# One core, attention and an expert layer: idle products moved to the head of TensorE's queue, one DMA for the last part of q, and new tables of order, engine and buffer

## The chip, the core and the metric

The kernel runs on one core of one Trainium2 chip. The metric is the time of one execution on the device in microseconds. Five engines work side by side, each through its own queue in order: PE (matrix products; its weight loads are listed as PEld), DVE, ACT, POOL (elementwise work), and SP, which here only issues DMAs. A queue whose next instruction waits holds back all that stands behind it.

## What is computed

```python
def _attn_ref(q, k, v):                      # q, k, v: (4, 8, 1152, 64)
    q_pool = q.reshape(B, H, S // 2, 2, D).mean(axis=3)
    scores = (1 / sqrt(D)) * np.matmul(q_pool, k.transpose(0, 1, 3, 2))
    scores = scores - np.max(scores, axis=-1, keepdims=True)
    attn = np.exp(scores)
    attn = attn / (np.sum(attn, axis=-1, keepdims=True) + 1e-09)
    return np.matmul(attn, v)
def _moe_ref(x, w_in, w_out):                # x: (2304, 512), 512 -> 2048 -> 512
    h = x @ w_in
    g = np.where(h > 0.0, h, np.exp(np.minimum(h, 0.0)) - 1.0)
    return g @ w_out
```

The weights come as float64 and are decoded on the chip.

## The kernel before, in words

There are four units, one for each batch, and each has four pairs of heads. A pair has nine score steps (two heads by four tiles of 128 pooled rows, and one of 64 rows from each head). A step is: `scores` on PE into the PSUM tile `s`, of which there is one; `biggest` on DVE, which reads `s`, finds the row maximum and writes `ep`; `expo` on ACT; `recip` (two operations on one column) on DVE or POOL. So the next `scores` waits until `biggest` has read the last one.

After that a step goes one of two ways. In a "split" pair (eleven of sixteen) the numbers are turned into two float16 parts, `phi` (hb, on ACT, POOL or DVE) and `plo` (DVE), DMAs transpose them, and `pv_split` multiplies them with v. In the others PE transposes `ep` (`turn`), ACT or DVE copies it out (`out_act`), and `pv` multiplies in float32. The first two pairs are "plain" as well: q and k stay float32, `q_twice` adds the two q rows of a pool, PE transposes them (`flip_turn`) and `flip_out` copies them out. For the other pairs `q_sum`, `hi` and `lo` make float16 halves.

The expert layer works on half a unit at a time (256 and 320 rows): `xlo` ends its input, 16 groups of products `m1_all` give h, six elementwise steps (`neg`, `ex`, `em`, `join`, `gh`, `gl`) give g, and `m2_all` makes the output, which `oe` copies out and `od` stores. Before that the weights are decoded on DVE (`dec`, three operations, 32 times) and split in two parts (`w_hi`, `w_lo`).

None of this runs in loops on the chip. The program makes 2691 tasks, and the table `ORDER` gives the order in which they are written out: `943v` is task 943 on DVE (p is PE, a ACT, g POOL, s a DMA on SP). What stands in front of a task on the same letter is what that engine does first. Many tasks can run on more than one engine, and the letter picks one. `SLOTS` says which buffer of its kind each value gets. The durations that `plan.add` is given are for the search that made the tables; with the tables written out they reach no instruction.

At the head of the kernel: `load_k` on SP, `load_qa` twice and `load_qb` (two DMAs, one for each head) on ACT's queue; `q_twice` three times on DVE, the third for `load_qb`'s part; `flip_turn` and `flip_out`; the first `scores`. Task 0 is `warm`, six products of the identity with itself, whose result nobody reads.

Of the kernel before, what the change touches and what calls it, by code (L numbers as in the profile page):

```python
# [37 lines left out]
411v 430g 41g 483p 484v 44a 359s 445p 446a 456p 468p 469a 304s 412p 473p 457a 295v 466p 474v 298s
498a 499g 467a 46p 447p 315v 47v 311v 413a 475a 519p 284s 448a 476v 297a 464p 454p 504p 48a 520v
449v 465a 49g 424p 485a 52a 300v 455a 505a 303s 509p 500p 510v 306v 481p 317a 487p 482a 502p 477p  # L40
555p 501a 50s 511a 488a 302a 503a 521a 470p 556v 478a 24s 55s 542p 479p 557a 480a 525p 471a 526a
308s 51s 318s 425a 506p 305v 286v 543v 515p 489p 507a 426v 508v 472v 486v 287a 490v 369s 532p 516a
307a 558g 559p 533v 522v 517p 523p 527p 491p 544a 524a 518a 565p 310v 56v 492a 493p 534a 53g 566v
371v 54s 59a 494a 567a 538p 578p 573p 560a 528a 513p 495v 569p 539a 574a 579v 57s 360s 550p 570a
320v 43s 375s 563p 561p 514a 562a 564a 551a 60a 601p 546p 571p 535g 568g 548p 536p 602v 61p 322a
361v 547a 364s 588p 512g 529p 572a 580a 62v 63a 67a 603a 589v 537a 530a 614p 64v 365s 377v 581v
615v 575p 531v 576v 312a 323v 577v 65s 70s 582p 605p 637p 590a 66s 545v 583a 604g 549a 606a 68g
638v 594p 607p 608a 609p 324p 584p 585a 610a 69s 616a 540p 647p 611p 366v 325v 541a 595a 648v 373a
596p 586p 618p 587a 326p 649a 367v 624p 552p 597a 327v 639a 625v 328g 683p 626a 612v 650v 591v 640v
613v 684v 362v 592p 651p 72s 619a 593a 652a 645p 653p 655p 354s 656a 685a 75a 646a 620p 660p 621a  # L50
553a 661v 654a 329v 598p 670p 687p 330v 599a 554v 600v 617g 71g 628p 632p 344s 662a 629a 633a 671v
74a 641p 643p 630p 644a 622p 631v 627v 623v 686g 73s 76a 350s 693p 58s 363a 379s 694v 634p 663v
355s 356v 331g 332g 333v 672a 635v 642a 368a 334g 335g 336g 688a 691p 729p 657p 730v 695a 658a 689p
706p 731a 636v 659v 697p 664p 77p 1831v 690a 692a 665a 666p 674p 707v 78v 668p 716p 669v 673v 676p
698a 675a 667a 717v 701p 696g 708a 677a 79a 337v 357v 349s 733p 699p 678p 679a 700a 83a 718a 702a
734a 739p 680p 732v 740v 681v 719v 80v 710p 714p 735p 712p 713a 741a 715a 736a 752p 682v 338a 753v
352v 703p 84g 765p 704a 711a 709g 705v 766v 722p 747p 754a 88s 723v 374s 345s 755v 742v 1832v 737p
743p 756p 775p 776v 81s 82s 748a 744a 745p 758p 358a 757a 738a 759a 339g 340g 351v 724p 746a 720p
721a 777a 767a 85s 760p 761a 1833p 1834v 798p 725a 799v 90s 749p 376v 1837a 380s 762p 750a 1838v
778g 788p 783p 800a 789v 751v 353a 771p 378a 726p 784a 727a 763v 764v 341v 811p 769p 728v 801g 779p  # L60
781p 790a 770a 89g 796p 772a 773p 812v 806p 780a 86g 87v 768g 92a 824p 782a 807a 792p 774a 91s 785p
825v 381v 342g 791g 797a 813a 826a 793a 832p 804p 802p 815p 93a 814v 827v 803a 805a 816a 828a 347v
833v 1839p 834a 382v 819p 817p 820a 842p 794p 786a 818a 821p 835v 843v 787v 1840a 94a 346v 850p
836g 95p 1853p 844a 830s 838s 96v 829v 1867p 795a 384v 348a 831s 822a 97g 845v 101a 1835v 1841a
1842a 98v 1907v 1843v 383a 851v 99s 1868a 1869a 1854a 1855a 837v 823v 106s 1856a 808p 809v 810v
1908v 385v 860p 846a 852a 343g 861v 839s 1846p 386p 848s 1844g 104a 102g 1857v 853v 1858a 108s
1909p 868p 1870v 862a 1910v 847v 1859g 1881p 869v 387v 105v 863v 1847a 1848a 849s 1849g 388g 1845g
1913a 1850v 1871v 854a 389v 107v 100s 1888p 1889a 1890a 870a 1860p 1861a 1862a 1874p 103s 855v
1914v 878p 1851a 1863a 1864v 864a 840p 856s 1852g 1929p 879v 390a 857s 109s 871g 1875a 391v 392g
872g 865v 1876a 867s 906p 1891a 841a 1877a 907v 866s 1878v 393v 110a 1865a 880a 881g 1901p 874s  # L70
1892v 1879a 886p 111a 112a 394a 873v 887v 882a 395v 1895p 858p 875s 896p 859a 888a 883v 113p 908a
1866g 1872a 1893a 114v 115g 897v 396g 1896p 884s 885s 116v 889v 1930a 124s 1911v 1894v 914p 876p
909g 890a 1902p 397v 891v 898a 1882a 1931a 877v 1883a 1932g 892s 915v 1933v 1884g 910a 893s 1880g
1943p 912s 1934a 932p 916a 1885v 1935g 894p 117s 1950p 911v 899v 933v 398a 399v 917g 913s 900a 902s
895a 119a 118s 901v 918a 934a 903s 1836v 1951a 1873v 400a 1952a 919v 1922p 1923a 1924a 942p 1903p
920s 1953a 1944a 120v 1945a 1946a 921s 401v 943v 1897p 924p 121s 935v 936g 1925a 1947v 904p 1954v
944a 1886g 922p 1887g 925v 950p 1948a 1926v 402a 905a 1957p 1936p 923a 926a 937v 938s 1949v 122a
951v 939s 968p 1964p 952a 1937a 1938a 126s 927v 928v 403v 929v 945v 946g 1927a 1939a 1940v 969v
1941a 930s 1942g 1928g 931s 123v 1904p 947v 948s 953g 125g 129a 1965a 1958a 1905a 1966a 970a 954a
# [258 lines left out]
def attention_moe_kernel(  # L338
# [9 lines left out]
    nc = tc.nc  # L348
# [59 lines left out]
    def dve(n):  # L408
        return Port(1.08 * n + 75.0)
# [974 lines left out]
```

## Time and profile before

| | us |
|---|---|
| median of 3 runs | 742.1 (742.02 to 743.98) |
| the profiled execution, its own time | 742.65 |
| its span, first to last instruction | 740.9 |
| PE busy | 717.3 (97%) |
| DVE busy | 625.0 (84%) |
| ACT busy | 560.6 (76%) |
| POOL busy | 338.0 (46%) |

The span is told from the first instruction of the program to its last; 1.75 us of the execution lie around it. A busy PE is not a PE at its peak: products overlap, and their ends are modelled. What shows whether PE has work is the idle time before its instructions, and what ended it.

### The profile page before, as it was taken

The page shows a single profiled execution, that of the slowest core. Times are in us where ns is not written, and L with a number is a line of the kernel's source. Part 1 is how long each engine was busy: PE and PEld are TensorE (multiplying, and loading weights), DVE is VectorE, ACT ScalarE, POOL GpSimd, SP SyncE. Part 2 cuts the span into 40 slices and gives each one's busy share as a digit, 9 for nine tenths or more (in the row PEclk, how much of TensorE's full clock was granted, in tenths as well). Part 3 has the DMA queues.
Part 4 walks back from the last instruction along what each step waited for, and adds up shares of the span by engine and source line. Part 5 has one row for each costly group of instructions (what it writes and reads, how often), then busy time and mean ns, then how long its engine had stood idle before and what let it go on. Part 6 is the DMA issues. An engine that isn't in the chain of part 4 may idle for free.

```text
span 740.9 us, 19632 instructions
## 1 busy us (share of the span) xinstructions
PE 717.3 (97%) x7905; PEld 478.8 (65%) x7905; DVE 625.0 (84%) x1098; ACT 560.6 (76%) x974; POOL 338.0 (46%) x385
## 2 busy tenths in 40 slices
PE   5899998999999999999999999999999999999997
PEld 4577776877565555775676566786665665865753
DVE  6999999999998998879898879899988989875330
ACT  3899997998998887777688766889788564752651
POOL 1322455466626633376465554354646452440430
PEclk9999999999999999999999999999999999999999
DMA  8787834577999998999999999899899998793001
GB/s 304 287 228 251 247 119 105 142 135 160 171 179 207 178 204 169 211 181 174 213 171 208 189 205 181 163 162 209 173 189 194 188 162 137 139 139 64 30 1 36
DMA packets 310971, 126.01 MB, mean 170 GB/s; under 512 B 286304, under 2 KB 288352, under 8 KB 310880
## 3 DMA queue, kind: packets, MB, share of 16 engines
q1 hardware_dynamic: 310432, 124.16, 82.4%
q8 instruction: 62, 1.02, 0.6%
q10 hardware_dynamic: 448, 0.59, 0.2%
q14 instruction: 29, 0.24, 0.1%
HBM read 45.09 MB, written 4.72 MB: 67 GB/s over the span
## 4 chain that ended last, share of the span: by engine, by line
PE 47%; DVE 3%; ACT 2%; issue 1%; DVEq 0%; ACTq 0%
PE r L1310 16%; PE r L1229 14%; PE r L1119 6%; PE s L956 4%; PE s L970 3%; PE r L1101 1%; DVE ep L985 1%; PE r L1067 1%; ACT ep L991 1%; PE s L961 0%; DVE ep L1045 0%; DVE tmp L1265 0%; DVE x L1207 0%; DVE g L1291 0%; ACT hb L1042 0%
## 5 line engine op out<-in xcount | busy, mean ns | idle before, releaser
L991 ACT ACTIVATE ep<-ep,wk 128x1152 f32<-128x1152 f32 x136 | 170.4, 1254 | 45.7 <-DVE ep L985 40.5
L1229 PE MATMUL r<-x,wi 128*128 128x256 f16 (+1 forms) x1536 | 196.6, 286 | 1.5 <-DVE tmp L1265 1.5
L985 DVE TENSOR_SCALAR_CACHE_REDUCE ep<-s,sm 128x1152 f32<-128x1152 f32 x122 | 172.3, 1412 | 13.0 <-PE s L970 9.2
L1229 PEld LDWEIGHTS <-wi 128*128 128x128 f16 x1536 | 147.6, 98 | 43.6 <-issue 6.1
L1310 PE MATMUL r<-wo,g 128*128 128x512 f16 (+1 forms) x864 | 174.9, 380 | 0.1
L1045 DVE SCALAR_TENSOR_TENSOR ep<-ep,wk,hb 128x1152 f16<-128x1152 f32 x99 | 146.0, 1478 | 6.7 <-ACT hb L1042 4.7
L1310 PEld LDWEIGHTS <-g 128*128 128x128 f16 (+1 forms) x864 | 73.3, 100 | 83.8 <-issue 4.7
L956 PE MATMUL s<-kT,qT 128*128 128x512 f16 (+3 forms) x420 | 82.9, 328 | 4.3 <-DVE ep L985 3.3
L1119 PEld LDWEIGHTS <-v 128*64 128x64 f16 x2970 | 77.8, 110 | 11.4 <-issue 10.5
L1119 PE MATMUL r<-pT,v 128*64 128x128 f16 (+1 forms) x2970 | 84.4, 215 | 0.3 <-DVE tmp L1265 0.3
L1283 POOL TENSOR_TENSOR g<-tmp,g 128x320 f16<-128x320 f32 (+1 forms) x61 | 68.1, 1118 | 36.0 <-ACT g L1279 34.4
L499 POOL TENSOR_SCALAR wk<-wk 128x1 f32<-128x1 f32 x68 | 31.2, 459 | 114.3 <-ACT ep L991 93.9
L1042 ACT ACTIVATE hb<-ep,wk 128x1152 f16<-128x1152 f32 x50 | 62.3, 1249 | 17.3 <-POOL wk L1010 8.2
L1036 POOL TENSOR_SCALAR hb<-ep,wk 128x1152 f16<-128x1152 f32 x34 | 44.3, 1303 | 56.6 <-DVE wk L1001 29.6
L1265 DVE SCALAR_TENSOR_TENSOR tmp<-r,tmp 128x320 f32<-128x320 f32 (+1 forms) x96 | 51.5, 551 | 21.5 <-POOL tmp L1250 11.5
L1242 ACT ACTIVATE tmp<-r 128x320 f32<-128x320 f32 (+1 forms) x96 | 45.1, 480 | 23.0 <-PE r L1229 14.7
L1245 ACT ACTIVATE tmp<-tmp,us 128x320 f32<-128x320 f32 (+1 forms) x96 | 57.8, 610 | 2.0 <-DVE us L1184 0.5
L956 PEld LDWEIGHTS <-qT 128*128 128x128 f16 (+1 forms) x420 | 33.9, 100 | 37.4 <-issue 13.7
L970 PE MATMUL s<-kT,qT 64*128 64x512 f16 (+1 forms) x280 | 49.6, 391 | 0.9 <-DVE ep L985 0.9
L1077 ACT ACTIVATE pT<-r 128x384 f32<-128x384 f32 x96 | 43.7, 498 | 8.7 <-PE r L1067 8.4
L1067 PE MATMUL r<-ident,ep 128*128 128x128 f32 x333 | 47.3, 283 | 2.3 <-DVE x L1134 2.3
L1287 POOL TENSOR_SCALAR g<-tmp 128x320 f16<-128x320 f32 (+1 forms) x42 | 28.8, 686 | 39.5 <-DVE tmp L1265 39.5
(163 smaller groups left out, 1044.0 us busy)
## 6 DMA issues: line engine op xcount, KB each, us to landing
v<-in_v_dram SPq DMA_DIRECT2D x16, 576.0 KB, 4.3
k<-in_k_dram SPq DMA_DIRECT2D x15, 576.0 KB, 4.5
g<-in_moe_w_in_dram SPq DMA_DIRECT2D x15, 512.0 KB, 7.2
q<-in_q_dram SPq DMA_DIRECT2D x15, 512.0 KB, 4.3
g<-in_moe_w_out_dram SPq DMA_DIRECT2D x15, 512.0 KB, 5.4
out_dram<-tmp SPq DMA_DIRECT2D x16, 256.0 KB, 3.0
qT<-qT SPq DMA_DIRECT2D x28, 144.0 KB, 3.0
pT<-hb SPq DMA_TRANSPOSE x99, 3.6
```

Of the source, the lines that this page charges most:

```text
L956: nc.tensor.matmul(s.ap[rows, c, 0:n], pr.qT.ap[:, 1 - c % 2, j, rows], keys[h][c], start=first[c], stop=not first[c] and c < 2, skip_grou ...
L970: nc.tensor.matmul(s.ap[rows, c, 0:512], pr.qT.ap[r, c, j, rows], keys[h][c][r], start=first[c], stop=not first[c], skip_group_check=True,)
L985: nc.vector.tensor_scalar(e_(), s.ap.rearrange("p a b -> p (a b)")[:, 0:S], -0.5 / float(D) ** 0.5 if pr.plain else pr.sm.ap[:, 12:13], No ...
L991: nc.scalar.activation(out=e_(), in_=e_(), func=AF.Exp, bias=nm.ap[:, 0:1], scale=-1.0, accum_out=nm.ap[:, 1:2],)
L1042: nc.scalar.activation(out=hb.ap, in_=e_(), func=AF.Copy, scale=nm.ap[:, 1:2])
L1045: nc.vector.scalar_tensor_tensor(out=e16(), in0=e_(), scalar=nm.ap[:, 1:2], in1=hb.ap, op0=ALU.mult, op1=ALU.subtract)
L1067: nc.tensor.transpose(tp.ap[:, c * 128:(c + 1) * 128], e_()[:, (j + c) * 128:(j + c + 1) * 128], ident)
L1119: nc.tensor.matmul(half(h), pr.v16.ap[:, h, order[c], e], p, start=(j + c == 0), stop=(j == 2 and c == NCH - 1), skip_group_check=True,)
L1229: nc.tensor.matmul(hp.ap[:, f * n:(f + 1) * n], w_in16[g][:, a, c, (f0 + f) * 128:(f0 + f + 1) * 128], x16.ap[:, e, c, g0:g0 + n], start=( ...
L1245: nc.scalar.activation(out=en.ap[:, :m], in_=en.ap[:, :m], func=AF.Exp, scale=us.ap[:, 8:9])
L1283: nc.gpsimd.tensor_tensor(out=l, in0=gv, in1=h, op=ALU.subtract)
L1310: nc.tensor.matmul(op.ap[r0:r0 + tn, :], gt[qd].ap[:, a, fi, o:o + tn], w_out16(f // 2)[:, e, f % 2, :], start=(i < 128 // tn), stop=(i >= ...
```

## The change

Four things change. `warm` has seven products instead of six and stands first in PE's order, where it stood behind six `flip_turn` and two `scores`. `load_qb` issues one DMA for both heads where it issued two. `ORDER` is another table: the same 2691 tasks in another order, 376 of them on another engine. `SLOTS` is another table. Two durations given to `plan.add` change too, and reach no instruction.

```diff
 ORDER = """
-2s 1s 11p 4a 16v 299s 9p 3a 314s 13v 5a 12a 10a 19v 17p 7p 283s 18a 414p 22s 288s 8a 301v 23s 316v
-370s 294s 415v 14p 15a 427p 285v 20p 21a 428v 429a 0p 437p 435p 289s 431p 27p 34g 416a 31v 290v
...
+0p 4a 16v 1s 2s 3a 13v 11p 299s 5a 7p 9p 17p 314s 12a 10a 283s 18a 8a 14p 19v 20p 22s 288s 414p
+301v 15a 316v 285v 415v 427p 289s 370s 416a 21v 31g 428v 290v 422p 420p 418p 23s 437p 438v 423a
...
         def load_qb():
-            for h in range(2):
-                nc.scalar.dma_start(
-                    out=q32.ap[64 * h:64 * h + 64, 2 * u.nt],
-                    in_=q[b, 2 * p + h, 2 * u.s0 + 256 * u.nt:][0:128].rearrange("(p r) d -> p r d", r=2),
-                )
+            nc.scalar.dma_start(
+                out=q32.ap[:, 2 * u.nt].rearrange("p r d -> p (r d)"),
+                in_=q[b, 2 * p:2 * p + 2, 2 * u.s0 + 256 * u.nt:][:, 0:128].rearrange("h (p r) d -> h p (r d)", r=2),
+            )
...
     def warm():
-        for i in range(6):
+        for i in range(7):
             nc.tensor.matmul(idle.ap[:, 0:128], ident, ident, start=True, stop=True)
```

In the two first lines of each table: 299, 314, 283 load the first three blocks of w_in; 301, 316, 285 are their `dec`; 414 and 427 are the first two `scores`, 415 and 428 their `biggest`; 16, 13, 19 are `q_twice`; 21 is the `flip_out` of q's last part.

## Rows read from the trace of the kernel before

**Rows 1.** Busy time by stretch: length, then each engine's busy us, granted clock, DMA.
```profile
0.00:20.00 20.00, 12.02 (x61) 8.47 (x61) 13.01 (x23) 7.41 (x12) 2.70 (x9) 1.00 0.90 310
20.00:213.00 193.00, 184.21 (x1973) 136.19 (x1974) 187.88 (x362) 179.27 (x334) 89.83 (x90) 0.99 0.72 183
213.00:303.00 90.00, 88.90 (x1024) 54.11 (x1023) 80.62 (x133) 72.48 (x118) 41.21 (x52) 1.00 1.08 188
303.00:741.00 438.00, 432.14 (x4851) 280.05 (x4849) 343.52 (x583) 301.40 (x511) 204.24 (x234) 1.00 0.83 154
```

**Rows 2.** Timeline of PE and DVE where the score task 924 starts: start, duration, instruction.
```profile
211.93 1.41 DVE L985 TENSOR_SCALAR_CACHE_REDUCE ep<-s,sm 128x1152 f32<-128x1152 f32 x1
213.41 0.59 PE L956 MATMUL s<-kT,qT 128*128 128x512 f16 x2
```

**Rows 3.** Timeline of DVE, the first 12 us; idle time and its releaser in brackets.
```profile
8.20 0.29 DVE L655 TENSOR_TENSOR kn<-q 128x128 f32<-128x128 f32 x1 [1.27 <-DMA q<-in_q_dram]
8.41 0.42 DVE L820 TENSOR_SCALAR tmp<-h 128x512 uint32<-128x512 uint32 x1
11.99 1.35 DVE L985 TENSOR_SCALAR_CACHE_REDUCE ep<-s 128x1152 f32<-128x1152 f32 x1
```

**Rows 4.** First DMA issues on the timeline, and their median time from issue to landing.
```profile
1.63 0.43 SPq L805 DMA_DIRECT2D h<-in_moe_w_in_dram  x1
1.65 1.16 ACTq L593 DMA_DIRECT2D q<-in_q_dram  x2
...
h<-in_moe_w_in_dram SPq DMA_DIRECT2D x1, 512.0 KB, 6.3
q<-in_q_dram ACTq DMA_DIRECT2D x2, 32.0 KB, 5.9
```

**Rows 5.** Timeline of PE, first 15 us, and POOL's last instruction on the identity.
```profile
1.00 0.29 POOL masks.py:199 TENSOR_SCALAR_AFFINE_SELECT ident<-ident 128x128 f32<-128x128 f32 x1
6.02 1.30 PE L624 MATMUL r<-ident,k 128*128 128x128 f32 x5 [6.02 <-DMA k<-in_k_dram]
8.96 2.08 PE L935 MATMUL s<-kT,qT 64*128 64x512 f32 x4
13.49 1.13 PE L935 MATMUL s<-kT,qT 64*128 64x512 f32 x4 [1.50 <-DVE ep L985]
14.43 0.38 PE L941 MATMUL s<-kT,qT 64*128 64x128 f32 x2
```

**Rows 6.** Groups of DVE instructions by line and shape: count, busy us, mean ns.
```profile
L1080 DVE COPY pT<-r 128x384 f32<-128x384 f32 x12 | 6.5, 550 | 2.9 <-PE r L1067 2.9
L655 DVE TENSOR_TENSOR kn<-q 128x512 f32<-128x512 f32 x3 | 2.1, 690 | 4.7 <-DMA q<-in_q_dram 4.7
L579 DVE TENSOR_TENSOR q<-q 128x576 f32<-128x576 f32 x4 | 3.0, 752 | 0.0
L499 DVE TENSOR_SCALAR wi<-wi,wk 128x1024 f16<-128x1024 f32 x1 | 0.8, 753 | 0.0
L850 DVE SCALAR_TENSOR_TENSOR wi<-wi,wk,wi 128x1024 f16<-128x1024 f32 x4 | 5.5, 1363 | 0.0
L1001 DVE RECIPROCAL wk<-wk 128x1 f32<-128x1 f32 x55 | 9.0, 164 | 1.9
L824 DVE SCALAR_TENSOR_TENSOR wi<-g,tmp 128x512 uint32<-128x512 uint32 x13 | 9.5, 728 | 0.4
```

**Rows 7.** Timeline of POOL and DVE around 119 us.
```profile
119.05 2.44 POOL L856 TENSOR_TENSOR wi<-wi,wi 128x1024 f16<-128x1024 f32 x1
119.54 2.50 DVE L824 SCALAR_TENSOR_TENSOR wo<-g,tmp 128x512 uint32<-128x512 uint32 x1
```

**Rows 8.** Waits of DVE between 213 and 303 us: sum, times, longest.
```profile
DVE ep L1045 <- ACT hb L1042: 2.4, 3, 1.0
```

**Rows 9.** Two pieces of the chain that ended last: start, duration, products.
```profile
633.38 10.59 PE r L1229 x96
713.33 23.55 PE r L1310 x132
```

More of the change, by code (lines that the diff above doesn't have):

```diff
@@ L38 @@
[L38 to L55, printed above, removed]
@@ new lines @@
+1222p 1232p 2131a 2132a 2211v 1239v 1241s 2192v 1245v 1246g 1262a 1252p 1263v 1223a 2160a 2161g
+1253v 2212a 1254a 1233v 2133v 2134v 2135g 195s 1247v 1240s 2162v 2163g 2164g 1248s 2144p 2221p
+2222a 2223a 2224a 2225v 2226g 2145a 2172p 187v 2227v 188s 1255v 2146a 2147a 1256a 1278p 1258s 2136g
+2148v 2149g 2173a 2193p 2214p 1249s 2127v 1279v 2194a 189s 2150v 2213v 2228p 1270p 2195a 2248p
+1257v 2215a 2216a 2217g 2196a 2197v 2218v 1259s 1264g 2235p 1266s 1280a 2174a 2175g 1265v 2198a
+1267s 193s 1271v 2229a 2230a 2242p 2231g 1281v 1282g 2219g 2220g 2199g 1272a 2232v 1273v 1274a
@@ new lines @@
+272p 2383g 2384v 1626v 1609s 2428v 1633a 2450p 273v 1634v 1618s 259s 1647p 1648v 2385a 2403a 1659a
+2404a 2405v 1660v 1627s 278a 279v 1635s 1661a 1619p 1620v 2386v 274g 275g 1639p 1628s 1662v 2451a
+2415p 2416a 2406a 2408p 2335a 2417a 2452a 1636s 1640v 2458p 2407g 276s 1663s 1675p 2436p 2418v
+2419v 1637p 2453v 2454v 1664s 1665p 277s 2409a 2410a 1649a 1650v 1651g 1641a 1642v 2411v 2412v
+2413a 1643g 280s 1676v 1652v 2414g 1644v 2437a 2438a 1653s 1667p 1668v 1677a 1654s 1645s 2443p
+2420a 2421g 1678g 2459p 1646s 1638v 2439v 2440v 2441a 2442v 1679a 1681s 1693p 1694v 2429p 1669a
@@ new lines @@
+1720a 1739p 1740v 1737p 1785p 1738v 2477v 2478p 2479v 1749a 1750v 1741a 2460p 2482a 1786v 1764s
+2483v 1765p 1763s 1751g 1742v 2467a 1743a 1753s 2468s 1752v 2461a 1745s 1766v 1767a 1744v 1768v
+2480v 1754s 2475s 1769a 1770v 1771s 1787a 1788g 2512p 2491p 2484p 1793p 2505p 1789v 1794v 2492a
+2513a 2514a 2515a 1775p 2485a 1795a 1772s 1796g 1773p 2481v 2516v 1776v 1774v 2486a 1746s 2462s
+2517a 2487v 1790v 2506a 2518v 1792s 2493a 1755p 2494a 2495v 1797v 1821p 1822v 2496a 2507a 2508g
+2498p 2533p 2488v 1798v 1799s 2489g 1777a 1823a 1824v 1825a 1800s 1811p 1812v 2509v 2510a 1756a
@@ new lines @@
+2490g 2511g 2519p 2520a 1791s 1827s 2534a 2521a 2522g 2526p 2499a 2500a 2501a 1826v 1828s 2497v
+1803p 1801p 1778g 1779a 2502v 2523v 1813a 1804v 2503g 1781s 1780v 1782s 1805a 2535a 2536v 2504g
+2537v 1806g 1829p 2540p 1807a 1808v 2527a 2528a 2529v 1814g 2538a 1809s 2541p 2546p 2547p 1810s
+1802a 2530v 2531a 2539v 1815g 1816v 1817s 1818s 2524a 2525v 2542p 2532g 1783p 1819p 2543p 1820v
+1830v 2553v 1784v 2552v 2554p 2555v 2556v 2548p 2549p 2558a 2559v 2581p 2602p 2550a 2609p 2637p
+2544a 2545s 2557v 2551s 2603a 2604a 2605g 2582a 2583a 2584a 2585v 2586a 2587v 2606v 2610a 2638a
@@ new lines @@
+2567p 2639a 2611a 2612v 2613v 2568a 2569a 2570g 2571v 2607g 2640a 2641v 2642a 2572a 2588p 2574p
+2608v 2665p 2573v 2575a 2576a 2577v 2614g 2615g 2589a 2560p 2578v 2590a 2591v 2579a 2580v 2561a
+2562a 2563a 2564v 2666a 2667a 2668g 2669v 2630p 2565g 2595p 2651p 2566v 2672p 2592v 2631a 2670a
+2671g 2593a 2632a 2594g 2643v 2633g 2596a 2597a 2598a 2634v 2635a 2616p 2599v 2600a 2617a 2623p
+2601v 2636v 2658p 2652a 2653a 2654g 2655v 2624a 2618a 2656a 2625a 2626v 2627v 2644p 2628a 2629v
+2619g 2620v 2659a 2660a 2661v 2621g 2622g 2645a 2646a 2647a 2648v 2649a 2662v 2678p 2679p 2680p
@@ L188 @@
+2657v 2663a 2664g 2650g 2681p 2682a 2684p 2685p 2686p 2687p 2688a 2689v 2690s 2683s 2673p 2674p
+2675p 2676a 2677s
 """
 SLOTS = """
[43 rows of a table removed]
[43 rows of a table added]
 """
@@ L607, in prep @@
             tq = [plan.add("ACT", 450.0 + h, lk - 10.0 + h, load_qa(h), (), [q32]) for h in range(2)]
-            tq.append(plan.add("ACT", 900.0, lk - 8.0, load_qb, (), [q32]))
+            tq.append(plan.add("ACT", 470.0, lk - 8.0, load_qb, (), [q32]))
         else:
@@ L707, in halves @@
             f, g = lo(dst_l, src, dst_h, j)
-            t = plan.add("DVE", Port(730.0, 730.0) if j == 1 else dve(n) + 35.0 * (j == 0), kl, f, [h], bufs, [("POOL", Port(pol(n), pol2(n)), g)] if CFG["PLP"] else [])
+            t = plan.add("DVE", Port(730.0, 730.0) if j == 1 else Port(*[0.5 * dve(n) + 17.5] * 2) if j == 0 else dve(n), kl, f, [h], bufs, [("POOL", Port(pol(n), pol2(n)), g)] if CFG["PLP"] else [])
             t.pen = CFG["PENH"]
@@ L758, in warm @@
     def warm():
-        for i in range(6):
+        for i in range(7):
             nc.tensor.matmul(idle.ap[:, 0:128], ident, ident, start=True, stop=True)
-    plan.add("PE", 1530.0, -1.0e9, warm, [], [idle])
+    plan.add("PE", 1820.0, -1.0e9, warm, [], [idle])
     for pr in pairs:
```

256 lines of the change are left out of this document (121 added, 135 removed), and 86 rows, old and new, of the table SLOTS.

## The prediction

> **What bounds the kernel now.** I read the busy times by stretch first, because the share of PE over the whole span (97%) hides a change of holder. From 20 to 213 us DVE is busy 187.9 of 193.0 us, so it idles 5.1; PE is busy 184.2 with 8.8 idle. From 213 to 303 us it is the other way round: PE idles 1.1 of 90 us, DVE 9.4. From 303 to the end PE idles 5.9 of 438 us, and some 4 of these are the end itself, the copy and the store behind the last product [rows 1]. So DVE holds the pace until about 213 us, and PE from there on.
>
> The place where the one hands over to the other can be seen: score task 924 starts on PE at 213.41, right behind the maximum (task 943, from 211.93, 1.41 long) that frees the one `s` tile [rows 2]. All later time is PE work, which the change leaves as it is (the same products). So the question is when task 924 can start with the new tables, and whether DVE lets PE run on after it.
>
> The head is a matter of its own. DVE waits for q's last part until 8.20, then decodes weights from 8.41 until the first maximum at 11.99; it does not wait for PE there [rows 3].
>
> **The sum is made against the profiled execution**: span 740.9, its own time 742.65, which is 0.55 over the median of 742.1. Its terms move task 924, and with it the end.
>
> *The DMA of q's last part.* Two issues take 1.16 us from 1.65 on ACT's queue, and a part lands 5.9 after its issue [rows 4]. One DMA is issued at 1.65 and lands about 7.55, if it takes as long (an estimate from these rows), so the third `q_twice` could run at 7.6. But the first decode needs its block of w_in, issued at 1.63 and 6.3 on its way [rows 4]: 7.93. The decode starts at 7.95 instead of 8.41: **-0.45 us**, between 0 (the larger DMA takes longer) and -0.45. ACT's queue is freed 0.6 earlier, which is worth nothing, since its first copy waits for PE.
>
> *Three decodes ahead of the first maximum.* In the new table DVE has 301, 316, 285, then maximum 415, flip copy 21, maximum 428. Before, the third decode stood between the two maxima. The order on DVE between two maxima matters, because the second `scores` needs `s`. From the end of the first maximum (11.99 and 1.35: 13.34) PE starts at 13.49 and is through at 14.43 + 0.38 = 14.81 [rows 3, 5], so DVE needs 1.5 us of other work there to miss nothing. A decode is (11.99 - 8.41) / 2 = 1.79 [rows 3] and filled it. The flip copy has 128 columns, and one of 384 takes 0.55 [rows 6]; I take 0.3. So DVE stands idle 1.2: **+1.2 us**, between 0.9 and 1.5. Nothing hides it, since DVE holds the pace.
>
> *Idle products.* They can start when the identity is written, at 1.3, and PE would wait for k until 6.02 in any case [rows 5]. Seven products are 14 records; the first five of PE's records took 1.30 us [rows 5], so 14 are an estimated 3.6 us, done at 4.9: they delay nothing, with 1.1 us to spare. What they may save: the first score products took 2.08, the same form later 1.13 [rows 5]. But the first maximum waits for the decodes, not for those products, so this is **0**; were PE the holder at the head it would be -0.95 for this one score. Removing six products from behind 14.43 is worth nothing either: PE waits there for the maximum.
>
> [...]
>
> *Order and engines up to task 924.* I counted in both tables what stands in front. On PE it is the same set, 222 tasks. On DVE in front of maximum 943 there were 209 tasks, and now there are 206. Fewer by two copies of `out_act` (0.55 each), one `q_twice` (0.69), one `q_sum` (0.75), one `w_hi` (0.75) and one `xdown2`; more by one `w_lo` (1.36), one `recip` (two operations near 0.16) and one `xb` [rows 6]. I set the last one of each list, both a few tenths, against each other. That is -(1.10 + 0.69 + 0.75 + 0.75) + 1.36 + 0.33 = **-1.6 us**. Its bounds are wide, because DVE's idle in that stretch (5.1) can be lost or doubled by other neighbours: -4 to +2, and I stay with the count, the one thing that is known.
>
> *POOL beside DVE.* At 119 us one DVE operation took 2.50 instead of the 0.73 of its group, and ended as POOL's 2.44 ended [rows 6, 7]. Before task 924 one `w_lo` leaves POOL, while `phi` on POOL goes from two to six. I take **0**, with plus or minus 1.8, one such overlap more or less.
>
> [...]
>
> *After task 924.* Waits of PE from 303 us on are 1.9 us apart from the end [rows 1]; no row tells which the new order keeps. I take 0, between -1.9 and +1.9. The end is the same in both tables: the last block of `m2_all`, its copy, its store. In front of the first block that needs the last products of w_in, seven others stood and now three; 132 products take 23.55 us, so three blocks of 12 are 6.4 [rows 9]. I cost it at nothing while the six elementwise steps stay under 6.4; every tenth over it is lost.
>
> The sum: -0.45 + 1.2 - 1.6 = -0.85. On the profiled 742.65 that is 741.8; on the median of 742.1, **741.3 us**.
>
> **The rivals.**
>
> *DVE keeps the pace until 303 us, and the kernel gets slower.* Between task 924 and score task 1114, the one that closes the stretch from 213 to 303 us, the new table puts eight DVE tasks more than the old, relative to the first count, three of them `recip`: at two operations near 0.16 each [rows 6] 2.5 us is the least, and I take it. And it takes two `m1_all` blocks out of PE's share, each 24 products, 10.59 / 4 = 2.6 [rows 9], and puts one `pv_split` in, for which I set 1.5 (54 short products, an estimate below that block): 3.7 less for PE. Together PE comes 6.2 us sooner upon DVE. DVE idled 9.4 there [rows 1]. So the point from which it decides: if more than 9.4 - 6.2 = 3.2 of those us of idle stay, every further microsecond is lost. For it: waits for things that other queues make (2.4 us for ACT's hb [rows 8]) do not vanish because DVE is late. Against it: ACT, too, has 13 tasks fewer in front of task 1114, and an engine that runs behind finds its inputs ready. With 5.9 of it left: +2.7, **744.0 us**. Chance 0.25.
>
> *The lead in the DVE stage is larger than the count, and the kernel gets faster.* In the middle of that stage (at score task 798) five DVE tasks less stand in front, not three. If the neighbours are better as well and half of DVE's 5.1 us of idle goes (-2.5), the sum is -3.3: **738.8 us**. For it: PE idled 8.8 there, and all of it is to be had once DVE comes sooner [rows 1]. Against it: what is left out early comes back before task 924, and 5.1 us in 193 is little to win from. Chance 0.27.
>
> *The change at the head doesn't do what it says.* The one DMA for both heads lands as late as the two, and the gain of 0.45 is gone: **741.8 us**. Chance 0.04.
>
> *POOL holds DVE up more often.* Two overlaps more before task 924 than before, 1.8 each [rows 6, 7]: **744.9 us**. For it: four more `phi` on POOL. Against it: one `w_lo` less, the operation of the row at 119 us. [...] Chance 0.04.
>
> **How the numbers follow.** The forecast has 0.40; its own range is 739.5 to 743.5, from the bounds of the two terms at the head, one overlap with POOL and the late waits. A measurement of this kernel can tell 0.3%, about 2.2 us, from no change: 739.9 and 744.3. Of the faster rival I put 0.24 below 739.9, of the forecast 0.05; above 744.3 lie 0.12 of the slower one, 0.03 of POOL's and 0.04 of the forecast. So faster 0.29, the same 0.52, slower 0.19. The range has to reach into both rivals: 738.0 to 745.5.
>
> **What would show it.** In the trace after: the third `q_twice` before 8.0 and a decode right behind it; an idle time of about 1.2 on DVE ahead of the second maximum, released by PE; task 924 about 0.85 earlier than 213.41; between 213 and 303 us DVE idle well under 9.4 and PE idle near 1. The prediction is wrong if DVE is no longer the busier engine before 213 us, or if PE shows several microseconds of waits for maxima between 213 and 303.

## The result

The changed kernel takes **747.5 us** (median of 5 runs, 746.17 to 749.47) against 742.1 before: a ratio of 1.0065, 95% interval 1.0045 to 1.0086. It is slower, by about 5 us, and the forecast of 741.3 with its range to 745.5 missed it. The profiled execution of after took 746.17 with a span of 744.4, 3.5 more than the span of before. The kernel before varies by itself: of its 35 runs timed beside e5, the five with a mean granted clock of 1.000 took 740.35 to 740.62 us, and the eleven at 0.995 or less 743.1 to 744.2.

| | before | after |
|---|---|---|
| median, us | 742.1 | 747.5 |
| profiled execution, its own time | 742.65 | 746.17 |
| its span | 740.9 | 744.4 |
| PE busy | 717.3 | 718.4 |
| DVE busy | 625.0 | 626.9 |
| ACT busy | 560.6 | 558.1 |
| POOL busy | 338.0 | 330.8 |

Busy times over the whole span tell little: the same work was done. The head tells more. First DVE of after on the timeline: the third `q_twice` waits for q's last part, and four microseconds later than in [rows 3] the decodes begin. The first maximum comes at 18.74 where it came at 11.99, and DVE then waits 2.45 for PE's second score.

```profile
12.21 0.29 DVE L654 TENSOR_TENSOR kn<-q 128x128 f32<-128x128 f32 x1 [4.95 <-DMA q<-in_q_dram]
12.42 0.42 DVE L819 TENSOR_SCALAR tmp<-h 128x512 uint32<-128x512 uint32 x1
...
18.74 1.34 DVE L984 TENSOR_SCALAR_CACHE_REDUCE ep<-s 128x1152 f32<-128x1152 f32 x1
...
22.75 1.36 DVE L984 TENSOR_SCALAR_CACHE_REDUCE ep<-s 128x1152 f32<-128x1152 f32 x1 [2.45 <-PE s L940]
```

PE of after, same view. The idle products end at 4.7. The transpositions behind them are as slow as in [rows 5] (nine in 2.15), and the second score takes 2.08, where it took 1.13 from 13.49 on.

```profile
1.35 3.36 PE L759 MATMUL r<-ident 128*128 128x128 f32 x14 [1.35 <-POOL ident masks.py:199]
6.36 2.15 PE L623 MATMUL r<-ident,k 128*128 128x128 f32 x9 [1.66 <-DMA k<-in_k_dram]
...
12.65 0.30 PE L623 MATMUL r<-ident,kn 128*128 128x128 f32 x1 [2.43 <-DVE kn L654]
12.88 1.38 PE L934 MATMUL s<-kT,qT 64*128 64x512 f32 x4
...
20.24 2.08 PE L934 MATMUL s<-kT,qT 64*128 64x512 f32 x4 [5.55 <-DVE ep L984]
```

The DMA view of after, first 20 us in 40 slices of half a microsecond: busy tenths of the 16 DMA engines, GB/s, and the packets of ACT's queue (q10).

```profile
DMA  0006889999999999983111000008799968999999
GB/s 0 0 0 97 253 335 347 389 402 366 333 376 391 407 395 413 393 316 125 48 46 44 20 8 0 0 0 82 270 356 345 174 181 266 344 328 344 422 385 238
...
q10 hardware_dynamic: 418, 0.59, 8.3%
```

From 9.5 to 11 us, when all else has landed, the DMA engines are busy by a tenth and move 44 to 48 GB/s where some 400 had gone before. Three such slices are some 70 KB, about the 64 KB of q's last part. A tenth of 16 engines is about two. In the same view of before no slice from 2.5 us on is under 6 tenths up to 12 us, and q10 has 448 packets. SP's queue stands still meanwhile: its next load needs the q buffer (it waits 9.0 us for DMAs of q, 2.8 in before), is issued at 12.53 (8.52 in before), and so every later load of the head comes late too.

The score task 924 starts 1.9 later than in [rows 2], not 0.85 earlier:

```profile
215.31 0.65 PE L955 MATMUL s<-kT,qT 128*128 128x512 f16 x3 [0.55 <-DVE ep L984]
```

### The profile page after: what moved, and what is told of

Its sections match the earlier page's. It is cut to its first block, busy times and chain, and to the rows that moved or that the text cites. A ratio compares the mean times of both kernels' runs of the same rounds, so it can differ in the third digit from the quotient of the medians.

```text
span 744.4 us, 19652 instructions
## 1 busy us (share of the span) xinstructions
PE 718.4 (97%) x7907; PEld 480.6 (65%) x7907; DVE 626.9 (84%) x1115; ACT 558.1 (75%) x974; POOL 330.8 (44%) x367
## 4 chain that ended last, share of the span: by engine, by line
PE 37%; DVE 4%; ACT 3%; POOL 3%; issue 2%; DMA 1%; POOLq 0%; ACTq 0%; DVEq 0%
PE r L1309 13%; PE r L1228 11%; PE r L1118 4%; PE s L955 3%; PE s L969 2%; DVE ep L984 2%; PE r L1066 1%; PE r L1100 1%; ACT ep L990 1%; DVE ep L1044 1%; POOL hb L1035 1%; POOL wk L1009 1%; DMA pT<-hb 1%; ACT hb L1041 0%; POOL g L1282 0%
## 5 line engine op out<-in xcount | busy, mean ns | idle before, releaser
L990 ACT ACTIVATE ep<-ep,wk 128x1152 f32<-128x1152 f32 x139 | 174.1, 1254 | 65.0 <-DVE ep L984 51.9
L1044 DVE SCALAR_TENSOR_TENSOR ep<-ep,wk,hb 128x1152 f16<-128x1152 f32 x99 | 148.9, 1509 | 8.7 <-POOL hb L1035 4.5
L1035 POOL TENSOR_SCALAR hb<-ep,wk 128x1152 f16<-128x1152 f32 x40 | 55.2, 1380 | 50.3 <-DVE wk L1000 20.1
L1282 POOL TENSOR_TENSOR g<-tmp,g 128x320 f16<-128x320 f32 (+1 forms) x53 | 59.0, 1118 | 30.3 <-ACT g L1278 28.9
L1041 ACT ACTIVATE hb<-ep,wk 128x1152 f16<-128x1152 f32 x46 | 57.4, 1249 | 19.6 <-POOL wk L1009 12.0
L499 POOL TENSOR_SCALAR wk<-wk 128x1 f32<-128x1 f32 x64 | 23.1, 361 | 107.4 <-ACT ep L990 101.3
L1249 POOL TENSOR_SCALAR tmp<-tmp,us 128x320 f32<-128x320 f32 (+1 forms) x37 | 26.6, 721 | 83.6 <-ACT tmp L1244 78.7
L1066 PE MATMUL r<-ident,ep 128*128 128x128 f32 x360 | 51.3, 283 | 0.2 <-ACT ep L990 0.2
```

The costliest lines, as they stand in the source:

```text
L990: nc.scalar.activation(out=e_(), in_=e_(), func=AF.Exp, bias=nm.ap[:, 0:1], scale=-1.0, accum_out=nm.ap[:, 1:2],)
L1035: nc.gpsimd.tensor_scalar(hb.ap, e_(), nm.ap[:, 1:2], 1.0, op0=ALU.mult, op1=ALU.mult)
L1044: nc.vector.scalar_tensor_tensor(out=e16(), in0=e_(), scalar=nm.ap[:, 1:2], in1=hb.ap, op0=ALU.mult, op1=ALU.subtract)
L1066: nc.tensor.transpose(tp.ap[:, c * 128:(c + 1) * 128], e_()[:, (j + c) * 128:(j + c + 1) * 128], ident)
L1282: nc.gpsimd.tensor_tensor(out=l, in0=gv, in1=h, op=ALU.subtract)
```

## Where the time goes, by milestones

Each line is one profiled execution (not always the middle one: that of after is the fastest of its five), in us: the fourth score (task 404), task 924, and what remains from there to the end of the span. The same products stand behind task 924 on PE in every kernel.

| kernel | third q_twice | second score | fourth score | task 924 | 404 to 924 | 924 to end |
|---|---|---|---|---|---|---|
| before | 8.20 | 13.49 | 20.14 | 213.41 | 193.3 | 527.5 |
| after | 12.21 | 20.24 | 27.24 | 215.31 | 188.1 | 529.1 |
| e1 two DMAs | 7.94 | 15.98 | 24.10 | 213.26 | 189.2 | 530.0 |
| e2 one DMA alone | 11.52 | 16.82 | 25.12 | 219.92 | 194.8 | 526.3 |
| e3 idle products alone | 8.30 | 13.59 | 21.72 | 213.88 | 192.2 | 528.0 |
| e4 tables alone | 8.48 | 16.70 | 24.93 | 212.96 | 188.0 | 529.1 |
| e5 decode between | 8.27 | 13.56 | 21.01 | 209.09 | 188.1 | 529.7 |
| e6 wait filled | 8.02 | 16.53 | 22.40 | 210.47 | 188.1 | 529.3 |
| e7 one DMA, 64 outermost | 7.56 | 15.58 | 22.76 | 210.76 | 188.0 | 529.7 |

So the change is three things: +7.1 up to the fourth score, -5.2 from there to task 924, +1.6 behind it. Together +3.5, the difference of the spans.

## The experiments

All ratios are to the kernel before, timed beside it on the same chip.

**The DMA.** e1 undoes it in the changed kernel, e2 does it alone in the kernel before.

```diff
 (e1, on after)
-            nc.scalar.dma_start(out=q32.ap[:, 2 * u.nt]..., in_=q[b, 2 * p:2 * p + 2, ...]...)
+            for h in range(2):
+                nc.scalar.dma_start(out=q32.ap[64 * h:64 * h + 64, 2 * u.nt], in_=q[b, 2 * p + h, ...]...)
```

> The changed kernel with one thing undone: load_qb is two DMAs again, one for each head. Theory (the merged DMA lands some 4 us later, runs on 2 of the 16 DMA engines, holds PE and DVE at the head and the next pair's q behind it, and most of the loss comes from there): queue q10 has about 448 packets again, the third q_twice is back near 8.0 to 8.2 instead of 12.21, task 924 moves from 215.3 to about 212 to 213, and the median falls from 747.5 to 742 to 744. Rival (the new tables lose the time themselves, by DVE's pace up to 303 us and by late waits of PE): the third q_twice is back near 8.2, but DVE, which holds the pace, loses the gain again by 213 us, and the median stays at 746 to 748.

Measured: 744.3, ratio 1.0020 (1.0006 to 1.0033). The third `q_twice` is back at 7.94, q10 at 448 packets. So the DMA is most of the loss, and some 1.5 us over before is left, a little more than the theory allowed.

> The kernel before with one thing done: load_qb is one DMA. Theory: q10 has about 418 packets, the third q_twice goes from 8.20 to about 12, and since in the old table it stands ahead of the decodes on DVE just as in the new, the whole head moves by about 4 us; up to 213 us DVE has 5 us of idle and can win little of it back, so the median goes from 742.1 to 745 to 746.5. Rival (the tables are at fault): the late q costs 1 us or less at the end, 742 to 743.

Measured: 747.7, ratio 1.0060 (1.0039 to 1.0081): that one edit in the kernel before costs as much as the whole change, and more than its theory had. Its `q_twice` of q's last part:

```profile
11.52 0.29 DVE L654 TENSOR_TENSOR kn<-q 128x128 f32<-128x128 f32 x1 [4.67 <-DMA q<-in_q_dram]
```

It is 3.3 later, and the fourth score 5.0: PE waits 6.04 for the later maximum, the granted clock of the first 20 us is 0.89 where before has 1.00 [rows 1], and the second score takes 2.08.

e7 keeps one DMA, with the same bytes in the same 512-byte packets (both DMA views count 256 packets from 512 bytes to under 2 KB in the first 20 us), and only turns the order in which it walks: pairs of rows outermost, heads inside.

```diff
 (e7, on after)
-                in_=q[...][:, 0:128].rearrange("h (p r) d -> h p (r d)", r=2),
+                in_=q[...][:, 0:128].rearrange("h (p r) d -> p h (r d)", r=2),
```

> The changed kernel, with the one DMA for q's last part read in another order: its outermost dimension is the 64 pairs of rows, with the two heads inside, instead of the two heads outermost. Bytes, packet size and count of DMAs are the same; the rows of the two heads come to lie in turns in q's last part, so the numbers of those score steps are mixed up (no work is left out). Theory (a DMA is dealt over the 16 DMA engines by its outermost dimension, and with 2 there it runs on 2 of them): the DMA's share stays high in the slices around 10 us instead of 0.1, q10 has about 432 packets, the third q_twice is at 8.5 or before instead of 12.21, and the time is that of the two DMAs, 743 to 745. Rival (one DMA of 64 KB in 512-byte packets is slow as such, or it is late behind the transfers in front): third q_twice at 11 or later, 746 to 748.

Measured: 742.3, ratio 1.0002 (0.9988 to 1.0015). The third `q_twice` runs at 7.56. The DMA view of e7, as above:

```profile
DMA  0007599999999999999699979999999999999999
...
q10 hardware_dynamic: 432, 0.59, 8.2%
```

No hole is left: from 2.5 us on no slice is under 6 tenths. So it is neither the one DMA nor the packet size: it is the outermost dimension of 2 on the DRAM side, the only side that e7 turns. With 2 there a tenth of the engines was busy in after, at 44 to 48 GB/s, and q's last part came at 12.21; with 64 it came at 7.56. How a DMA is dealt over the engines beyond these two walks no run shows. The packets fit: the counts 448 (two DMAs), 432 (the fast one) and 418 (the slow one) each leave 288 for the two large parts if 128 are of q's last part and 2 times 16, 16 and 2 are a small one from each engine that took part; that is an estimate from the three counts, not shown by a row.

**The idle products.** e3 puts seven at the head of PE in the kernel before; e4 takes the new tables with two DMAs, and six products back in their old place.

```diff
 (e3, on before)               (e4, on e1)
-2s 1s 11p ...  429a 0p 437p   -0p 4a 16v ...
+0p 2s 1s 11p ... 429a 437p    +4a 16v ... 415v 427p 0p 289s
-        for i in range(6):    -        for i in range(7):
+        for i in range(7):    +        for i in range(6):
```

> The kernel before with seven idle products first on PE, everything else as it was. Theory (they wait for nothing that PE needs and finish before k lands): first flip_turn still at 6.02 and its five products still near 1.30, the first scores at 8.96 still near 2.08 or up to 0.95 shorter, the first maximum at 12.0 as before since DVE decodes until then: 742.1, within 0.7. Rival (the clock's granted level is spent at the head and falls later, at about 13 us, as in the changed kernel): products between 13 and 24 us at half the clock, median 1 to 3 us over 742.1.

Measured: 744.5, ratio 1.0021 (1.0002 to 1.0041). The first five transpositions take 0.74 instead of 1.30 and the first score 1.13 instead of 2.08, so PE is ready sooner, waits 3.68 instead of 1.50 for the maximum, and then runs at a granted clock of 0.50 (16 to 20 us): its third score takes 2.08. The median lies with the rival, not the theory, though the interval hardly leaves 1.

> The two tables alone: the changed kernel with two DMAs for q's last part and with six idle products behind the second score, as they stood before. Theory: as the kernel with two DMAs, within 1 us (742 to 744), because the idle products decide nothing. Rival (the idle products first cost clock): 1 to 3 us faster than the kernel with two DMAs and the idle products first. Rival (the tables are at fault): 746 to 748.

Measured: 744.7, ratio 1.0027 (1.0014 to 1.0040), the same as e1. With the new tables it makes no difference which of these two places the idle products have.

**The third decode, and the clock.** e5 moves that decode back between the first two maxima; e6 leaves it and puts twenty idle products into PE's wait.

```diff
 (e5, on e1)                            (e6, on e1)
-301v 15a 316v 285v 415v 427p           -0p 4a 16v ... 288s 414p 301v
+301v 15a 316v 415v 285v 427p           +4a 16v ... 288s 414p 0p 301v
                                        -        for i in range(7):
                                        +        for i in range(20):
```

> The kernel with two DMAs (tables and idle products of the change) and one task moved: the third decode (285) stands between the first two maxima again, as before the change, not ahead of the first. Theory (the three decodes keep PE from its second score for 6 us, its clock falls, and DVE then waits 2.45 for that score and 1.03 for the next): PE waits some 4 us instead of 6.02 ahead of the second score, DVE waits less than 1 instead of 2.45 ahead of the second maximum, task 924 starts 1 to 2.5 us earlier than 213.26, and the median falls from 744.3 to 742 to 743.5. Rival (DVE wins the loss at the head back by 213 us anyway): task 924 within 0.5 of 213.26, median 744 to 745.

Measured: 741.7, ratio 0.9993 (0.9982 to 1.0005). Task 924 at 209.09, 4.2 earlier than in e1. Of this 3.1 arise up to the fourth score; the rest lies at 188 to 194 us, where the granted clock of e1's profiled run was 0.72 and that of e5's 1.00.

> The kernel with two DMAs and the idle products moved: twenty of them between the first score and the second, where PE waits 6 us for the first maximum; the three decodes stay ahead of that maximum. Theory (the fall of the granted clock behind that wait costs part of the hole): the granted clock stays at its upper level from about 10 us on, the second score's four products take 1.13 instead of 2.08, DVE's wait ahead of the second maximum falls from 2.45 to about 1.5 (the predicted 1.2 and what the extra products add), the next wait of 1.03 is gone: task 924 1 to 2 us earlier, median 742.5 to 743.5. Rival (the clock at the head doesn't matter): 744 to 745.

Measured: 741.9, ratio 0.9994 (0.9983 to 1.0005). Stretches of four microseconds of e1, then of e6 (length, busy us of PE, PEld, DVE, ACT, POOL, granted clock, DMA share, GB/s):

```profile
12.00:16.00 4.00, 0.02 (x2) 0.05 (x2) 3.93 (x6) 0.13 (x1) 2.93 (x2) 0.50 0.94 328
16.00:20.00 4.00, 4.00 (x14) 2.77 (x15) 1.55 (x4) 1.82 (x4) 0.00 (x0) 0.50 1.02 393
```
```profile
12.00:16.00 4.00, 4.00 (x37) 4.00 (x38) 3.93 (x6) 0.00 (x0) 2.94 (x2) 1.00 0.90 306
16.00:20.00 4.00, 3.68 (x25) 2.48 (x24) 2.29 (x7) 2.53 (x4) 0.00 (x0) 1.00 1.03 388
```

In e1 PE stands idle from 10 to 16 us and is granted 0.50 when its score comes; in e6 it keeps 1.00. DVE's wait ahead of the second maximum, e1 and then e6:

```profile
18.49 1.36 DVE L985 TENSOR_SCALAR_CACHE_REDUCE ep<-s 128x1152 f32<-128x1152 f32 x1 [2.45 <-PE s L941]
```
```profile
17.91 1.36 DVE L977 TENSOR_SCALAR_CACHE_REDUCE ep<-s 128x1152 f32<-128x1152 f32 x1 [1.68 <-PE s L933]
```

So the theories of e5 and e6 hold, and both kernels gained more than expected (task 924 comes 4.2 and 2.8 earlier than in e1). The decode in that place costs 3.1 at the fourth score; with the clock held at 1.00 (e6) 1.4 of it is left (22.40 against 21.01), and the rest came through the clock.

**Behind task 924.** In after PE waits from 213 to 738 us for this (total, times, longest):

```profile
PE s L955 <- DVE ep L984: 2.8, 5, 0.9
PE r L1228 <- ACT x L1127: 1.5, 1, 1.5
PE r L1228 <- DVE tmp L1264: 0.8, 2, 0.5
PE r L1228 <- DVE x L1130: 0.3, 1, 0.3
PE r L1309 <- POOL g L1282: 0.2, 1, 0.2
```

That is 5.6; the same view of before has 2.5. e8 tries to mend the second row (with the decode between, and eight products in PE's wait); e9 tries to mend the first by giving six tasks back from DVE to ACT, the engine that they had before, at the places that they have in the new order; e10 adds to e9 the small DMAs of q ahead of the large ones.

```diff
 (e8, on e5)                         (e9, on e5)
-2166a 2167a 1187a 2208a             -972v 1018v 1041v 1059v 1960v 2023v
+1187a 2187a ... 2166a 2167a 2208a   +972a 1018a 1041a 1059a 1960a 2023a
 (also 0p behind 414p, 8 products)   (e10, on e9: 5a ahead of 4a)
```

> The new tables with three mends: two DMAs for q's last part; the third decode between the first two maxima, with eight idle products between the first two scores to fill PE's wait; and the ACT copy 1187, whose PSUM buffer PE waits 1.5 us for at 384 us, ahead of the copies 2166 and 2167 that wait for PE. Theory: head -2.5 to -3.5 us against the kernel with two DMAs (both holes of DVE gone), the wait at 384 us gone (-1 to -1.5): 740 to 742. Rival (after 213 us other waits take their place): 742.5 to 744.

Measured: 742.0, ratio 0.9996 (0.9983 to 1.0008); from task 924 to the end 529.6, no better than e5's 529.7. The wait of 1.5 is gone, and these stand in its place in part (PE's timeline, 360 to 400 us):

```profile
364.49 1.70 PE L1111 MATMUL r<-pT,v 128*64 128x128 f16 x54 [0.43 <-DVE tmp L1257]
...
390.40 1.80 PE L1221 MATMUL r<-x,wi 128*128 128x320 f16 x12 [0.34 <-DVE x L1123]
398.50 0.65 PE L948 MATMUL s<-kT,qT 128*128 128x512 f16 x3 [0.44 <-DVE ep L977]
```

> The kernel with two DMAs and the third decode between the maxima, and six tasks between score tasks 924 and 1114 given back from DVE to ACT, where they stood before the change: two conversions to float16 (972, 1018), two em (1960, 2023), two xb (1041, 1059). Theory (DVE's larger share in that stretch keeps PE waiting there: 1.73 us of PE idle where there were 1.10, and 2.2 us more from task 924 to the end): the stretch from 924 to 1114 shrinks by 0.5 to 1.2 us from 86.40, PE's waits for DVE at 242, 252 and 278 us are gone or halved, and the median goes from 741.7 to 740.5 to 741.3. Rival (PE waits there for single results that are late for another reason, and the stretches behind 1114 take any gain back): 741.4 to 742.

Measured: 746.7, ratio 1.0060 (1.0045 to 1.0074). Both expectations were wrong: PE idles 5.95 us from 213 to 303, not 1.7. ACT had a quarter of that stretch free (64.4 of 90 us busy), and still its queue, at these places in the order, was wrong for them. Waits of DVE from 205 to 300 us in e9 (total, times, longest):

```profile
DVE ep L1037 <- ACT hb L1034: 5.1, 4, 2.6
DVE tmp L1257 <- POOL tmp L1242: 3.1, 2, 2.6
```

In e5 these are 0.8 and 0.4. ACT's free time is mostly one wait, for DVE's next maximum (15.7 of it in e5, 16.5 in e9); what was put into its queue behind such a wait came late, and then DVE waited for it (the 5.1), and PE for DVE (1.7 and 1.4 for maxima from 200 to 300 us).

> The same kernel with one thing more: on ACT's queue the two DMAs for q's last part go out ahead of the two large ones for the rest of q. Theory (DVE holds the pace up to 213 us and starts to decode as soon as q's last part and w_in are there): the third q_twice runs at 7.6 to 8.0 instead of 8.27, everything up to task 924 comes 0.3 to 0.5 us earlier, at most 0.5 us at the end. Rival (the large parts come 0.6 later, and flip_turn, the first score and the first maximum with them): no gain, or up to 0.6 us later.

Measured: 749.1, ratio 1.0086 (1.0067 to 1.0104), most of it e9's. What it adds is at the head: with the small parts in front the first large part's `q_twice` runs at 8.60 instead of 4.63, and the second score at 16.05 instead of 13.40. Both expectations failed: the third `q_twice` runs behind the late large ones, later than 10.1, and the loss up to task 924 is 1.6 (212.31 against 210.71).

**Versions without the slow form.** In e12 and e13 the one DMA walks in the fast order, and the copy behind the transposition (`flip_out`) puts the columns of the two heads back in place. e12 has the new tables with the decode between, e13 the old ones; e14 moves in the old tables one decode behind a maximum, e15 is e14 with the fast DMA.

```diff
 (e12, e13: load_qb as in e7, and for q's last part of the first pair)
+    o, i = o.rearrange("d (h p) -> d h p", h=2), i.rearrange("d (p h) -> d h p", h=2)
 (e14, on before)
-352v ... 705v ... 766v
+705v ... 766v 352v
```

> The new tables with q's last part by one DMA whose outermost dimension is the 64 pairs of rows (the copy behind the transposition puts the columns of the two heads in their places again, so the result is the whole one), and with the third decode between the first two maxima. Theory (with neither the slow form of the DMA nor the decode ahead of the maximum the change's DMA is worth its 0.45 and the tables win some 4 us before task 924 and lose some 2 behind it): third q_twice at 7.5 to 7.7, decode at about 7.95, task 924 at 208 to 209.5, median 740.5 to 742 where the kernel before has 742.2. Rival (the copy with columns in turns is slow, or the clock falls as it did in other runs and takes 1 to 2 us): 742 to 744.

> The kernel before with only q's last part by one DMA in that fast order. Theory (the DMA term of the prediction, -0.45, holds where the DMA is dealt over all engines): third q_twice at 7.5 to 7.8 instead of 8.20, decode some 0.4 earlier, and 0 to 0.5 us at the end: 741.6 to 742.2. Rival (one DMA as such costs): 743 or more.

Measured: e12 741.6, ratio 0.9989 (0.9975 to 1.0003); e13 741.5, ratio 0.9986 (0.9973 to 1.0000). With 64 as the outermost dimension the decode of e13 starts 0.12 earlier than in [rows 3], not the 0.4 that was expected, on the timeline of DVE:

```profile
8.08 0.29 DVE L661 TENSOR_TENSOR kn<-q 128x128 f32<-128x128 f32 x1 [1.05 <-DMA q<-in_q_dram]
8.29 0.42 DVE L826 TENSOR_SCALAR tmp<-h 128x512 uint32<-128x512 uint32 x1
```

By the ratio e13 is 1.0 faster than before, with an interval that reaches to no change; the 0.12 does not give that, and its profiled run had a granted clock of 1.00 from 20 to 213 us where before has 0.99 (see below). e12's profiled run started its decode at 8.07 and lost 3.0 against e5 up to task 924: its third score took 2.08 (at 18.17; 1.13 in e5), and its granted clock was 0.98 from 20 to 213 us and 0.72 from 188 to 194, where e5's was 1.00 in both.

> The kernel before with one task moved: the decode (task 352) that stands on DVE at 117.64 us, where two of its operations take 1.40 and 2.50 beside POOL's w_lo instead of 0.69 each and PE then waits 2.26 and 0.72 us, goes behind the next maximum (766). Theory (that one meeting of DVE and POOL, with PE's waits and the fall of the clock behind it, is what the new tables win before task 924): PE is busy some 14 of the 15 us from 113 to 128 instead of 11.48, the clock doesn't fall at 123.84, task 924 starts 3 to 5 us before 213.41, and the median falls by 2 to 4.5 us to 738 to 740. Rival (DVE, busy 97% of that stage, gives the gain back before task 924, and the new tables won it by their many other moves): task 924 within 1 us of 213.41, median 741.5 to 742.5.

> The same, with q's last part by one DMA in the fast order (64 pairs of rows outermost). Theory: the two gains add, 737.5 to 739.5, task 924 at 208 to 210. Rival: 741 to 742.

Measured: e14 741.9, ratio 0.9985 (0.9970 to 1.0000), task 924 at 213.16: the rival. e15 741.5, ratio 0.9981 (0.9969 to 0.9993), task 924 at 212.58: the rival again, and not to be told from e12, e13 and e14. In e14 the meeting with POOL is only moved: two operations of the decode take 1.04 and 1.49 where they take 0.42 and 0.69 elsewhere, and PE waits 2.65 for what DVE does behind them. PE idles 3.2 us from 113 to 128 in e14 and 3.5 in e15, as it did before.

```profile
120.20 1.04 DVE L812 TENSOR_SCALAR tmp<-g 128x512 uint32<-128x512 uint32 x1
121.27 1.49 DVE L813 SCALAR_TENSOR_TENSOR tmp<-g,tmp 128x512 uint32<-128x512 uint32 x1
```
```profile
124.01 3.43 PE L1059 MATMUL r<-ident,ep 128*128 128x128 f32 x15 [2.65 <-DVE wk L995]
```

## Why the prediction was wrong

*The DMA of q's last part: the step that failed.* The prediction had -0.45, with 0 as the worst, on the condition that one DMA lands as long after its issue as one of the two did [rows 4]. It did not: 4.0 later at `q_twice` in after, 3.3 in e2. The bound was taken from the duration of a DMA of another shape, and none above zero was set, though the diff shows the two heads moving to the outermost place. The rival "doesn't do what it says" went only as far as 0, too. Nor was ACT's queue freed 0.6 earlier: the one issue took 1.11 us there (0.60 in the fast form, e7). The fast form measured -0.12 at the decode in the old table (e13) and -0.38 at `q_twice` in the new one (7.56 in e7, 7.94 in e1).

*Three decodes ahead of the first maximum: the mechanism was right, the size not.* A hole released by PE is there, 2.45 instead of 1.2, and a second one of 1.03 in e1. The 1.2 came from a score at a granted clock of 1.00 ([rows 5], 14.81); behind a wait of 5.55 us PE ran it at 0.50 in after (2.08 instead of 1.13). In e6, at 1.00, DVE's wait is 1.68, and some 0.4 of it is the extra products' (the score starts 0.50 behind the end of the maximum, 0.14 in e1), so without the fall of the clock the 1.2 was about right. From the third `q_twice` to the fourth score after takes 3.1 more than before: the hole of 2.45, 0.3 for the flip copy, 0.95 for a meeting with POOL, less 0.6 for a `q_twice` that stood there. The meeting was overlooked: in after the moved decode's last operation runs beside a `q_twice` of the next pair on POOL and takes 1.64, where the same one before it took 0.69.

```profile
16.62 3.32 POOL L654 TENSOR_TENSOR kn<-q 128x512 f32<-128x512 f32 x2 [15.32 <-DMA q<-in_q_dram]
17.18 1.64 DVE L823 SCALAR_TENSOR_TENSOR wi<-g,tmp 128x512 uint32<-128x512 uint32 x1
```

*Idle products: 0 held for PE's queue* (done at 4.7, the estimate was 4.9), and for the tables of the change (e4 as e1). In the old table they cost perhaps 1.5 (e3). They do not hold the clock through the wait for the first maximum (5.55 us in after, 6.02 in e1): it was granted 0.50 from 14 to 18 us in after and from 12 to 20 in e1.

*Order up to task 924: -1.6 became -5.2, and POOL beside DVE was not 0.* The way was right, the size wrong. Some 1.4 of the 5.2 is luck of the trace of before, whose granted clock was 0.50 from 124 to 126 us. e13 has the old tables, the same waits of PE there and no fall, and took 191.9 from its fourth score to task 924 (before 193.3, the new tables 188.0 to 188.1 where the granted clock is 1.00 on the way). So the tables' own gain is some 3.8, near the end of the term's bounds (-4 to +2), and -5.2 lies beyond it. For PE it lies mostly in one place. From 113 to 128 us, before, e13 and after (columns as in the windows above):

```profile
113.00:128.00 15.00, 11.48 (x105) 8.71 (x103) 14.37 (x26) 9.63 (x20) 8.84 (x7) 0.89 0.53 130
```
```profile
113.00:128.00 15.00, 11.48 (x123) 8.63 (x123) 14.76 (x27) 10.98 (x23) 8.79 (x7) 1.00 0.52 130
```
```profile
113.00:128.00 15.00, 14.92 (x166) 11.96 (x165) 14.35 (x29) 14.31 (x31) 9.64 (x9) 1.00 0.47 117
```

PE idles 3.5 of these 15 us with the old tables and 0.1 with the new. That is where POOL and DVE meet. The prediction priced one meeting at 1.8 and set the change in them to 0 [rows 7]; its row had one of three stretched operations, and that one ended some 0.5 behind POOL's, not with it. The two others of before, with the POOL operation beside the first, and PE's two waits behind them:

```profile
113.19 2.38 POOL L699 TENSOR_TENSOR kn<-k,kn 128x1152 f16<-128x1152 f32 x1
114.00 2.18 DVE L693 SCALAR_TENSOR_TENSOR qn<-q,sm,qn 128x576 f16<-128x576 f32 x1
118.10 1.40 DVE L821 SCALAR_TENSOR_TENSOR tmp<-g,tmp 128x512 uint32<-128x512 uint32 x1
```
```profile
122.39 0.52 PE L1067 MATMUL r<-ident,ep 128*128 128x128 f32 x3 [2.26 <-DVE x L1134]
123.63 0.94 PE L956 MATMUL s<-kT,qT 128*128 128x512 f16 x3 [0.72 <-DVE wo L985]
```

The three took 2.18, 1.40 and 2.50 where the same forms take 0.81, 0.69 and 0.69 elsewhere: 3.9 more. On DVE, which held the pace before, that is what the count missed. From the fourth maximum to task 943, before and then after:

```profile
21.79:211.93 190.14, 181.48 (x1961) 134.66 (x1960) 185.09 (x357) 176.56 (x330) 89.59 (x90) 0.99 0.72 183
```
```profile
28.93:213.84 184.91, 180.26 (x1962) 133.66 (x1960) 179.94 (x355) 174.92 (x332) 87.75 (x90) 1.00 0.76 188
```

DVE is busy 5.1 us less, and its idle time is 5.0 in both (in e13 184.5 busy and 4.3 idle). PE idles 8.7 before and 4.7 after, so both engines then stand near their limit. The 3.9 of meetings and the 1.6 of the count make 5.5, an estimate near that. So the rival with more meetings had the sign wrong. Whether the meetings are the cause of PE's wait is not shown: e14 moved the decode and did not remove them, with 2.19 for the first operation there and 1.04 and 1.49 for the decode's.

*After task 924: 0 became +1.6* (2.2 in e5), inside the bounds of 1.9 or close to them. The rival "DVE keeps pace until 303 us" did not come true: DVE's idle from 213 to 303 is 7.1 in after, more than twice the point from which it was to decide, and yet the stretch from task 924 to 1114 took 86.4 instead of 89.8: 3.4 less, where the prediction had 3.7 less of PE work. The loss is in single waits of PE (5.6 in sum where there were 2.5), and two tries to trade them away won nothing (e8, e9).

The signs of the prediction's last part read thus: `q_twice` before 8.0 failed and named the cause at once; the hole ahead of the second maximum was there; task 924 and the idle times behind it were off as told. Of the two signs of being wrong the first came true: from 20 to 213 us PE was busy 187.4 us in after and DVE 185.4. The second did not: PE's waits for maxima between 213 and 303 us sum to 1.4.

## What to carry to other kernels

Before two DMAs are made one, look at the outermost dimension on the DRAM side: here the 64 pairs of rows belonged there, not the 2 heads (third `q_twice` at 7.56 against 12.21), and where the rows then land in another order, let a copy that runs anyway put them right (0.28 us in e12 as in e5). A bound for a changed transfer must come from a row of the same shape, or have no upper end. Of a stall in the trace, price the whole chain behind it (the operation, who waits for it, and the clock after the wait: in before 2.26 and 0.72 us, then 0.50 granted), not the stretched operation alone; and an engine's idle share does not say that its queue can take work without making others wait (e9: 746.7 where e5 has 741.7).

## What was not expected of the hardware

- A DMA of 64 KB with 2 as its outermost dimension ran at 44 to 48 GB/s in after and came 3.3 (e2) to 4 us (after) later than the two; with 64 there it came 4.7 earlier than that (7.56 against 12.21).
- PE's granted clock fell to 0.50 in or behind waits of 2.43 to 6.02 us at the head (after, e5, e3, e1), and a score of 1.13 took 2.08. The wait alone did not settle it: 2.25 at the head of e13 left it at 1.00, and waits of 2.26 and 0.72 us were followed by 0.50 from 124 to 126 us in before, and the same two by 1.00 in e13. The same 3.36 us of idle products were followed by transpositions at 0.13 us each in e1 and at 0.24 in after, with 1.00 granted in both from 4 to 8 us. With 0.72 granted from 188 to 194 us (e1) the new tables took 1.1 more from the fourth score to task 924 than with 1.00 there (e5).
- Twenty idle products in the wait kept the clock at 1.00 from 8 to 24 us (e6), and eight in the shorter wait of e8 at 1.00 over the first 20; seven at the start did not (e1: 0.50 from 12 to 20 us).
